# Retention and two FFNs on one core: from the ninth unit on, one attention visit per unit in place of two

## The chip, the cores and the metric

The kernel runs on one core of a Trainium2 chip. The metric is device time of one execution in microseconds (us); before the change it was 1397.0 us, the median of 3 runs (1395.46 to 1397.63).

## What is computed

Everything is fp32. Retention over 8 batches, 8 heads, 576 positions, 64 features a head, then two feed-forward networks over the 4608 tokens of 512 features:

```python
scores = scale * np.matmul(q, k.transpose(0, 1, 3, 2))
gamma = 1.0 - 2.0 ** (-5.0 - np.arange(H))
Dmat = np.where(rel >= 0, gamma[:, None, None] ** rel[None, :, :], 0.0)
x = np.matmul(scores * Dmat, v)          # (B, H, S, D), then tokens x 512
h = x @ w_in                             # 512 -> 2048
x = (h * np.cos(h)) @ w_out              # 2048 -> 512
h = np.maximum(np.maximum(x @ w1, x @ w2), x @ w3)   # 512 -> 768, three times
out = h @ w_out2                         # 768 -> 512
```

## The kernel before

**Tiling.** Tokens are cut into 9 blocks of 512. A *unit* is one block and one pair of heads, so there are 36 units (`NUNIT`), four per block, counted from 0; retention of a unit is worked in chunks of at most 128 positions. The decay factors are taken apart: `v` is scaled by a growing factor beforehand (`att_scale`, GpSimd, for units 3 to 7 ScalarE), the outputs by a falling one afterwards (`att_decay`, VectorE), so that the scores need a 0/1 mask only (`att_mask`, VectorE). What lies before a chunk comes in through a running sum of key-value products: `att_products` (TensorE) makes a unit's products, `att_states` copies them out of PSUM (ScalarE) and adds them to the carried sum (GpSimd). `att_out` makes the outputs: the *inner* part, masked scores times `v` (line 667), and the *outer* part, carried sum times `q` (line 679), both into one PSUM bank `po`. `att_scores` (line 600) makes the scores into two banks `sc`. A unit's data lie in one tile `u`, loaded by `att_load` on SP's queue.

**The FFN beside it.** The FFN products are split in two fp32r halves (`high`, a cast on ScalarE; `low`, the rest, on VectorE, line 399) and use seven products in place of eight (A11, S1, A12, S2, A22, S4, S3). In this phase every FFN product is one *slot* of 12 matmuls of 256 columns (line 422). Each block takes 14 slots; two groups of four weight columns. After a slot its sum is taken by ScalarE (`copy`) or, for S4 and S3, by VectorE (`plus`, line 475). A gate (`gate`: two ScalarE steps, lines 526 and 536, and two VectorE steps, lines 530 and 539) follows each half group. `low` of a block's S2 is issued in the block's slot 1 (slot 14j of block j), two slots before TensorE reads it; those of S4 and S3 two slots later.

**The order** is written out by hand. `at(n, fn, turn)` puts a step on the agenda n slots ahead; `tick()` ends a slot, after its 12 matmuls and its own copy or `plus` have been issued, and then runs what is due: first the steps put down as `AHEAD`, in the order in which they were put down, later the others (`LATER`), in that order too. Each engine's queue is in order. The first 17 slots (`LEAD`) hold the lead-in of weights and units 0 to 7 (`NLEAD` is 8); the slots of the FFN are counted from 0 after them. Unit n from 8 on begins at slot `start_of(n)` = 3 + 11(n-8)//3, so three or four slots apart (3, 6, 10, 14, 17, ...). Units 8 and 9 have loads and scaling of their own.

**The attention steps of a unit n before** (`att_unit`): load at start-4, scaling at start-1, scores at start (`AHEAD`), mask at start+1; at start+5 the visit (`AHEAD`): key-value products of unit n+1 (`att_products(n + 1)`), then inner and outer outputs of unit n (`att_out(n)`), and in the same slot the states of n+1; at start+6 the decay of unit n. So TensorE breaks its FFN matmuls twice per unit: for scores, and one or two slots after the next unit's scores for products and outputs.

After the blocks' first FFN half follow, on the same agenda, the second half of the input weights, the output product, and the second FFN; the change touches none of them. There are 8 PSUM banks: one holds a sum for the whole phase, up to three belong to FFN groups, four to attention (`sc` twice, `kv`, `po`).

Of the kernel before, what the change touches and what calls it, by code (L numbers as in the profile page):

```python
# [39 lines left out]
def chunks_of(j):  # L40

    t0 = j * NB
    cut = (-t0) % S
    segs = [(0, cut), (cut, NB)] if 0 < cut < NB else [(0, NB)]
    out = [(a, min(CH, e - a)) for s, e in segs for a in range(s, e, CH)]
    full = [c for c in out if c[1] == CH]
    short = [c for c in out if c[1] < CH]  # L50
    assert len(short) in (0, 2) and all(n == CH // 2 for _, n in short)
    order = full + short
    col = {a: sum(n for _, n in order[:i]) for i, (a, _) in enumerate(order)}
    return [(a, n, col[a], (t0 + a) % S) for a, n in out]
# [52 lines left out]
def retention_ffn(ctx: ExitStack, tc: tile.TileContext, att, w_in, w_out, w123, w_out2, cst, out):  # L107
# [9 lines left out]
    def w14(name, dt=F32R):  # L117
        shape = [128, 7, 2, HB] if dt == F32R else [128, 7 * NB]
        return wpool.tile(shape, dt, tag="w", name=name)
# [4 lines left out]
    def bank(name):  # L124
        return ps.tile([128, NB], F32, tag="b", name=name)
# [21 lines left out]
    AHEAD, INSIDE, AFTER, LATER = range(4)  # L147

    def at(n, fn, turn=LATER):
        agenda.setdefault(slot[0] + n, [[], [], [], []])[turn].append(fn)  # L150
# [398 lines left out]
    units = {}  # L549
    quarters_of = {}  # L550

    def order_of(n):
        return divmod(n, NPAIR)

    def att_load(n):
        j, hp = order_of(n)
        w = w14(f"u{j}_{hp}", F32)
        units[n] = {
            "qk": w[:, : 2 * NB].rearrange("p (a n) -> p a n", a=2),
            "kv": w[:, 2 * NB : 4 * NB].rearrange("p (a n) -> p a n", a=2),  # L560
            "tv": w[:, 4 * NB : 4 * NB + NTV],
            "ret": w[:, 4 * NB + NTV : 6 * NB + NTV].rearrange("p (a n) -> p a n", a=2),
            "sums": w[:, 6 * NB + NTV : 6 * NB + NTV + 4 * D].rearrange("p (k n) -> p k n", n=D),
            "w": w,
        }
        nc.sync.dma_start(out=w[:, : 4 * NB + NTV], in_=att[j, hp])
# [3 lines left out]
    def att_scale(n):  # L570

        u = units[n]
        v = u["kv"][:, 1].rearrange("p (s d) -> p s d", d=64)
        if n in ON_ACT:
            for s in range(8):
                nc.scalar.mul(v[:, s], v[:, s], u["tv"][:, s : s + 1])
        else:
            nc.gpsimd.tensor_tensor(out=v, in0=v, in1=u["tv"].unsqueeze(2).to_broadcast([128, 8, 64]), op=ALU.mult)
        for _, m, c, pos in chunks_of(order_of(n)[0]):
            if m < CH and pos + m == S:  # L580
                s, p = divmod(c, CH)
                nc.gpsimd.memset(u["kv"][p : p + m, 0, s * CH : (s + 1) * CH], 0.0)

    def att_scores(n):
        u = units[n]
        ch = chunks_of(order_of(n)[0])
        u["sc"] = [bank(f"sc{n}_{e}") for e in range(2)]
        for s in range(NB // CH):
            sl = slice(s * CH, (s + 1) * CH)
            runs = sorted((c, a) for a, _, c, _ in ch if c // CH == s)  # L590
            for e in range(2):
                r = slice(64 * e, 64 * e + 64)

                a = runs[0][1]
                if len(runs) == 1:
                    q = u["w"][r, a : a + CH]
                else:
                    apart = runs[1][1] - a
                    q = u["w"][r, a : a + 2 * apart].rearrange("p (b d) -> p b d", b=2)[:, :, : CH // 2]
                nc.tensor.matmul(u["sc"][e][:, sl], u["qk"][r, 1, sl], q, start=True, stop=True)  # L600
# [20 lines left out]
    def att_products(n):  # L621

        u = units[n]
        ch = chunks_of(order_of(n)[0])
        kn, v = u["kv"][:, 0], u["kv"][:, 1]
        u["kv_sums"] = b = bank(f"kv{n}")
        for k, i in enumerate(grown(n)):
            s = ch[i][2] // CH
            for e in range(2):
                cols = slice(s * CH + 64 * e, s * CH + 64 * e + 64)  # L630
                nc.tensor.matmul(
                    b[64 * e : 64 * e + 64, k * D : (k + 1) * D], kn[:, cols], v[:, cols], start=True, stop=True
                )

    def att_states(n):

        u = units[n]
        j, hp = order_of(n)
        ch = chunks_of(j)
        of = grown(n)  # L640
        su = u["sums"]
        nc.scalar.copy(su[:, : len(of)], u["kv_sums"][:, : len(of) * D].rearrange("p (k n) -> p k n", n=D))
        before = carry[hp][(j + 1) % 2]
        u["state"] = {}
        for i, (_, m, _, pos) in enumerate(ch):
            if pos:
                u["state"][i] = before
            if i not in of:
                continue
            k = of.index(i)  # L650
            dst = carry[hp][j % 2] if i == len(ch) - 1 else su[:, k]
            if pos:
                nc.gpsimd.tensor_tensor(out=dst, in0=before, in1=su[:, k], op=ALU.add)
            elif i == len(ch) - 1:
                nc.gpsimd.tensor_copy(dst, su[:, k])
            before = dst

    def att_out(n):
        u = units[n]
        j, hp = order_of(n)  # L660
        ch = chunks_of(j)
        qT, v = u["qk"][:, 0], u["kv"][:, 1]
        po = u["po"] = bank(f"po{n}")
        for i, (a, m, c, _) in enumerate(ch):
            s = c // CH
            for e in range(2):
                nc.tensor.matmul(
                    po[64 * e : 64 * e + 64, a : a + m],
                    v[:, s * CH + 64 * e : s * CH + 64 * e + 64],
                    u["ret"][:, e, c : c + m],  # L670
                    start=i == 0,
                    stop=False,
                    skip_group_check=True,
                )
        for i, st in u["state"].items():
            a, m, _, _ = ch[i]
            for e in range(2):
                r = slice(64 * e, 64 * e + 64)
                nc.tensor.matmul(
                    po[r, a : a + m], st[r], qT[r, a : a + m], start=False, stop=True, skip_group_check=True  # L680
                )

    def att_decay(n):
        u = units.pop(n)
        j, hp = order_of(n)
        o = quarters_of.setdefault(j, {"name": f"x{j}", "n": NB})
        half = f"k{hp // 2 + 1}"
        if half not in o:
            o[half] = x4(f"{half}_x{j}", [2, NB])
        cuts = sorted({0, HB, NB, (-j * NB) % S} & set(range(NB + 1)))  # L690
        for lo, hi in zip(cuts, cuts[1:]):
            t, cc = divmod(lo, HB)
            g = CGS + hp * 9 + (j * NB + lo) % S // 64
            at_ = (hp % 2) * HB + cc
            nc.vector.scalar_tensor_tensor(
                out=o[half][:, t, at_ : at_ + hi - lo],
                in0=u["po"][:, lo:hi],
                scalar=cs[:, g : g + 1],
                in1=cs[:, CG + hp * HB : CG + hp * HB + hi - lo],
                op0=ALU.mult,  # L700
                op1=ALU.mult,
            )

    def att_visit(n):

        if n + 1 < NUNIT:
            att_products(n + 1)
        att_out(n)

    def att_unit(n, start):  # L710

        if n not in (NLEAD, NLEAD + 1):
            at(max(0, start - 1), lambda: att_scale(n))
        at(start, lambda: att_scores(n), AHEAD)
        at(start + 1, lambda: att_mask(n))
        if not n:
            at(start + 1, lambda: att_products(n), AHEAD)
            at(start + 1, lambda: att_states(n))
        at(start + 5, lambda: att_visit(n), AHEAD)
        if n + 1 < NUNIT:  # L720
            at(start + 5, lambda: att_states(n + 1))
        at(start + 6, lambda: att_decay(n))

    NUNIT = NBLK * NPAIR

# [74 lines left out]
    NLEAD = 8  # L800
# [13 lines left out]
    at(3, claim)  # L814
    at(4, lambda: lead_in(1, 0, nc.vector, nc.vector, SECOND))
    for n in range(NLEAD):
        att_unit(n, 2 * n + 1)
    at(13, lambda: lead_in(2, 0, nc.vector, nc.vector, SPREAD))
    at(16, lambda: lead_in(3, 0, nc.vector, nc.vector, SPREAD))
    build_in(block_of(0), 0, (10, 14, 15, 16), (10, 12, 14, 16, 17, 18, 19), xsd[0], nc.vector)  # L820
# [4 lines left out]
    def start_of(n):  # L825
        return 3 + (11 * (n - NLEAD)) // 3

    for n in range(NLEAD, NUNIT):
        if n > NLEAD + 1:
            at(max(0, start_of(n) - 4), lambda n=n: att_load(n))  # L830
        att_unit(n, start_of(n))
    per = 14
    for j in range(1, NBLK):
        build_in(block_of(j), per * j, (-11, -4, -3, -1), (-10, -8, -3, -1, 1, 1, 4), xsd[j], nc.vector if j == NBLK - 1 else nc.gpsimd)
# [32 lines left out]
    for i in range(4):  # L867
        n = endA + (10, 38, 66, 90)[i]
# [772 lines left out]
```

## Time and profile before

| | us |
|---|---|
| median of 3 runs | 1397.0 (1395.46 to 1397.63) |
| the profiled execution | 1396.5 |
| its span, first to last instruction | 1394.7 |
| TensorE busy in it | 1363.3 |
| VectorE busy | 1129.4 |
| ScalarE busy | 799.0 |
| GpSimd busy | 230.0 |

The retention phase lies in the first 313 us of the span. The profile is of one execution. Engines: PE is TensorE's matmuls, DVE is VectorE, ACT ScalarE, POOL GpSimd, SP the queue that issues loads and stores. A row of the timeline merges neighbouring instructions of a kind: start, length, engine, line, operation, output and inputs by tile name, shapes, count, and in brackets the idle time before it with what ended it. Matmuls are pipelined and the last one's end is modelled, so the time that a group costs TensorE is read from its start to the start of the next row and not from its length.

### The profile page before, as it was taken

How to read it: one execution, taken by the hardware profiler on the slowest of the kernel's cores; microseconds unless marked ns; L12 is line 12 of the kernel's file. 1: busy time of each engine (PE TensorE's matmuls, PEld its weight loads, DVE VectorE, ACT ScalarE, POOL GpSimd, SP SyncE). 2: the span in 40 equal slices, each digit the busy share in tenths (PEclk: the TensorE clock that was granted, in tenths of full speed). 3: DMA queues.
4: the chain of work that ended last, by engine and by line, in shares of the span. 5: the costliest groups of instructions: out<-in, count | busy, mean ns of one | idle time of the engine just before them, and what ended most of it. 6: DMA issues, size and time to landing. Idle time of an engine off the chain costs nothing.

```text
span 1394.7 us, 22899 instructions
## 1 busy us (share of the span) xinstructions
PE 1363.3 (98%) x8794; PEld 1175.4 (84%) x8794; DVE 1129.4 (81%) x1471; ACT 799.0 (57%) x1238; POOL 230.0 (16%) x259
## 2 busy tenths in 40 slices
PE   7899999999999999999999999999999999999998
PEld 5799999998888887888988888889878888888887
DVE  8988878989687789989879989577777567868884
ACT  6565565568677876666456556444544434444553
POOL 4455555730110000000011110100100000000000
PEclk9999999999999999999999999999999999999999
DMA  9679899988999975664577997343434476255633
GB/s 387 249 286 333 332 343 311 340 314 318 357 349 339 358 286 211 242 226 173 178 258 207 309 255 209 100 154 114 174 134 159 166 273 252 88 180 155 224 106 121
DMA packets 113085, 333.67 MB, mean 239 GB/s; under 512 B 9936, under 2 KB 18256, under 8 KB 107344
## 3 DMA queue, kind: packets, MB, share of 16 engines
q1 hardware_dynamic: 110096, 322.77, 63.9%
q0 software_dynamic: 2880, 9.44, 3.7%
q8 instruction: 69, 1.13, 0.3%
q14 instruction: 40, 0.33, 0.1%
HBM read 194.28 MB, written 137.89 MB: 238 GB/s over the span
## 4 chain that ended last, share of the span: by engine, by line
PE 55%; DMA 5%; DVE 3%; ACT 1%; issue 1%; SPq 0%; ACTq 0%; DVEq 0%
PE d_e L444 12%; PE d_g L976 11%; PE b_g L976 6%; PE b_e L444 6%; PE d_u L1506 5%; PE a_g L976 3%; PE a_e L444 3%; PE b_u L1506 2%; PE d_b L422 2%; PE a_u L1506 1%; DMA mqp<-ext 1%; PE b_b L422 1%; PE d_gs L976 1%; DMA gqp<-s_a 1%; DMA ar_b<-w 1%
## 5 line engine op out<-in xcount | busy, mean ns | idle before, releaser
L976 PE MATMUL d_g<-h_g,w_wo 128*128 128x512 f32 x512 | 157.9, 390 | 0.5 <-ACT o_g L999 0.5
L444 PE MATMUL in<-y,w_wi 128*128 128x512 f32 x672 | 153.0, 389 | 0.0
L444 PEld LDWEIGHTS in<-y,w_wi 128*128 128x128 f32 x672 | 125.9, 188 | 26.5 <-ACT s_a L1112 0.4
L943 DVE TENSOR_TENSOR l_g<-q_g,h_g 128x1024 fp32r<-128x1024 f32 x96 | 116.7, 1229 | 13.9 <-ACT h_g L936 9.5
L469 ACT ACTIVATE ext<-d_e 128x512 f32<-128x512 f32 x72 | 43.1, 599 | 143.1 <-PE d_e L444 143.1
L422 PE MATMUL d_a<-x_x,w_wi 128*128 128x256 f32 x864 | 117.3, 288 | 7.1 <-DVE w_wi L236 4.8
L936 ACT CAST h_g<-q_g 128x1024 fp32r<-128x1024 f32 x96 | 99.0, 1052 | 35.3 <-DVE q_g L927 22.9
L422 PEld LDWEIGHTS d_a<-x_x,w_wi 128*128 128x128 f32 x864 | 107.7, 192 | 12.3 <-DVE w_wi L236 5.0
L976 PEld LDWEIGHTS d_g<-h_g,w_wo 128*128 128x128 f32 x512 | 95.9, 188 | 20.6 <-ACT o_g L999 0.9
L539 DVE SCALAR_TENSOR_TENSOR s_a<-t_a,s_a 128x1024 f32<-128x1024 f32 x68 | 94.1, 1385 | 12.0 <-ACT t_a L536 12.0
L976 PE MATMUL d_g<-l_g,w_wo 128*128 128x512 f32 x256 | 99.8, 390 | 0.2 <-DVE l_g L943 0.2
L530 DVE SCALAR_TENSOR_TENSOR t_a<-s_a,t_a 128x1024 f32<-128x1024 f32 x68 | 88.5, 1303 | 14.2 <-ACT t_a L526 14.2
L526 ACT ACTIVATE t_a<-s_a 128x1024 int32<-128x1024 f32 x68 | 71.9, 1058 | 21.5 <-DVE s_a L1115 15.3
L536 ACT ACTIVATE t_a<-t_a 128x1024 f32<-128x1024 f32 x68 | 72.0, 1059 | 20.5 <-DVE t_a L530 20.2
L444 PE MATMUL d_e<-h_e,w_b 128*128 128x512 f32 x304 | 81.4, 390 | 0.8 <-DVE ext L473 0.8
L976 PE MATMUL b_g<-h_g,w_wo 128*128 128x512 f32 x256 | 79.2, 390 | 1.5 <-ACT h_g L936 1.5
L473 DVE TENSOR_TENSOR ext<-ext,b_e 128x512 f32<-128x512 f32 x36 | 24.7, 686 | 59.4 <-PE b_e L444 51.7
L444 PEld LDWEIGHTS d_e<-h_e,w_b 128*128 128x128 f32 x304 | 56.9, 188 | 12.9 <-DVE ext L473 1.2
L422 PE MATMUL b_a<-x_x,w_wi 128*128 128x256 f32 x432 | 60.6, 290 | 0.9 <-DVE x_x L399 0.9
L976 PEld LDWEIGHTS b_g<-h_g,w_wo 128*128 128x128 f32 x256 | 47.8, 188 | 12.1 <-ACT h_g L936 2.4
L422 PEld LDWEIGHTS b_a<-x_x,w_wi 128*128 128x128 f32 x432 | 55.3, 195 | 3.2 <-DVE x_x L399 1.1
L976 PEld LDWEIGHTS d_g<-l_g,w_wo 128*128 128x128 f32 x256 | 48.1, 188 | 11.0 <-DVE l_g L943 1.0
(371 smaller groups left out, 3322.4 us busy)
## 6 DMA issues: line engine op xcount, KB each, us to landing
u<-att SPq DMA_DIRECT2D x36, 1028.0 KB, 8.3
gqp<-s_a SPq DMA_DIRECT2D x64, 512.0 KB, 6.8
q_g<-gqp SPq DMA_DIRECT2D x64, 512.0 KB, 7.0
xsp<-x_x SPq DMA_DIRECT2D x56, 512.0 KB, 7.5
y<-xsp SPq DMA_DIRECT2D x56, 512.0 KB, 8.8
mqp<-ext SPq DMA_DIRECT2D x24, 512.0 KB, 4.1
st_b<-p_b SPq DMA_DIRECT2D x21, 512.0 KB, 6.4
w_b<-st_b SPq DMA_DIRECT2D x5, 1792.0 KB, 12.8
```

The lines of the kernel that those rows point to most:

```text
L422: nc.tensor.matmul(h[:, p * HB : (p + 1) * HB], a, b, start=first and p == 0 and i == 0, stop=i == len(terms) - 1, skip_group_check=True,)
L444: nc.tensor.matmul(dst, a, b, start=first and i == 0, stop=i == len(terms) - 1, skip_group_check=True)
L469: nc.scalar.activation(dst, b[:, :n], AF.Copy, scale=scale)
L473: nc.vector.tensor_tensor(out=dst, in0=dst, in1=b[:, :n], op=ALU.add)
L526: nc.scalar.activation(st["t"], s, AF.Copy, bias=0.25)
L530: nc.vector.scalar_tensor_tensor(out=r, in0=s, scalar=MOST_TURNS, in1=st["t"], op0=ALU.min, op1=ALU.subtract)
L536: nc.scalar.activation(r, r, AF.Sin, scale=TURN, bias=HALF_PI)
L539: nc.vector.scalar_tensor_tensor(out=s, in0=f32(st["t"]), scalar=-1.0, in1=s, op0=ALU.max, op1=ALU.mult)
L936: nc.scalar.copy(h, ts[i][q])
L943: nc.vector.tensor_tensor(out=lo, in0=t, in1=f32(h), op=ALU.subtract)
L976: nc.tensor.matmul(to, a, v[:, p].rearrange("p (b n) -> p b n", b=2) if half and n == 2 else v[:, :, r], start=first and k == 0 and p == 0 ...
L1506: nc.tensor.matmul(dst, a, v, start=first and p == 0 and i == 0 and (wide or mt == 0), stop=p == 2 and i == 2, skip_group_check=True,)
```

## The change

`att_out` is cut in two, `att_inner` and `att_outer`. A visit at slot `start` of unit n now holds, in this order, scores of n (from unit 8 on), inner outputs of n-1, key-value products of n, outer outputs of n-1. Units 0 to 7 keep their scores in a slot of their own and their visit in the slot in which it was (2n + 4, for unit 0 slot 2), with inner outputs now ahead of products. From unit 8 on decay of n-1, mask of n and states of n are put down for start+1, in this order in each engine's queue; before, decay stood at the unit's own start+6, which is one or two slots later than now, products and states at the unit before's start+5, which is one or two slots (products) or none or one slot (states) later. Scaling goes from start-1 to start-2, the load from start-4 to start-5. Outputs of the last unit get a visit of their own, at the slot where a unit 36 would begin.

```diff
-    def att_out(n):
+    def att_inner(n):
         u = units[n]
-        j, hp = order_of(n)
-        ch = chunks_of(j)
-        qT, v = u["qk"][:, 0], u["kv"][:, 1]
+        ch = chunks_of(order_of(n)[0])
+        v = u["kv"][:, 1]
         po = u["po"] = bank(f"po{n}")
         for i, (a, m, c, _) in enumerate(ch):
...
+
+    def att_outer(n):
+        u = units[n]
+        ch = chunks_of(order_of(n)[0])
+        qT, po = u["qk"][:, 0], u["po"]
         for i, st in u["state"].items():
...
     def att_visit(n):
 
-        if n + 1 < NUNIT:
-            att_products(n + 1)
-        att_out(n)
-
-    def att_unit(n, start):
+        if n >= NLEAD:
+            att_scores(n)
+        if n:
+            att_inner(n - 1)
+        att_products(n)
+        if n:
+            att_outer(n - 1)
+
+    def att_unit(n, start, visit):
 
         if n not in (NLEAD, NLEAD + 1):
-            at(max(0, start - 1), lambda: att_scale(n))
-        at(start, lambda: att_scores(n), AHEAD)
+            at(max(0, start - (1 if n < NLEAD else 2)), lambda: att_scale(n))
+        if n < NLEAD:
+            at(start, lambda: att_scores(n), AHEAD)
+        at(visit, lambda: att_visit(n), AHEAD)
+        if n:
+            at(visit + 1, lambda: att_decay(n - 1))
         at(start + 1, lambda: att_mask(n))
-        if not n:
-            at(start + 1, lambda: att_products(n), AHEAD)
-            at(start + 1, lambda: att_states(n))
-        at(start + 5, lambda: att_visit(n), AHEAD)
-        if n + 1 < NUNIT:
-            at(start + 5, lambda: att_states(n + 1))
-        at(start + 6, lambda: att_decay(n))
+        at(visit if n < NLEAD else visit + 1, lambda: att_states(n))
...
     for n in range(NLEAD):
-        att_unit(n, 2 * n + 1)
+        att_unit(n, 2 * n + 1, 2 * n + 4 if n else 2)
...
     for n in range(NLEAD, NUNIT):
         if n > NLEAD + 1:
-            at(max(0, start_of(n) - 4), lambda n=n: att_load(n))
-        att_unit(n, start_of(n))
+            at(max(0, start_of(n) - 5), lambda n=n: att_load(n))
+        att_unit(n, start_of(n), start_of(n))
+    at(start_of(NUNIT), lambda: (att_inner(NUNIT - 1), att_outer(NUNIT - 1)), AHEAD)
+    at(start_of(NUNIT) + 1, lambda: att_decay(NUNIT - 1))
```

## Rows read from the trace of the kernel before

**Rows 1.** The page, part 1: busy us (share of the span) and instructions of an engine.
```profile
PE 1363.3 (98%) x8794; PEld 1175.4 (84%) x8794; DVE 1129.4 (81%) x1471; ACT 799.0 (57%) x1238; POOL 230.0 (16%) x259
```

**Rows 2.** Waits of PE over the span: line, waited for, us, times, longest.
```profile
PE sc L600 <- DMA u<-att: 9.5, 2, 8.2
PE d_a L422 <- DVE w_wi L236: 4.8, 1, 4.8
PE d_a L422 <- DVE x_x L399: 2.2, 2, 1.8
...
PE b_a L422 <- DVE x_x L399: 0.9, 1, 0.9
```

**Rows 3.** Timeline of PE, 241 to 262 us: units 28 to 30, block 6.
```profile
244.49 1.16 PE L600 MATMUL sc<-u 64*128 64x128 f32 x16
245.58 1.70 PE L422 MATMUL b_a<-x_x,w_wi 128*128 128x256 f32 x12
247.21 0.69 PE L631 MATMUL kv<-u 128*64 128x64 f32 x16
...
249.63 3.13 PE L422 MATMUL d_a<-x_x,w_wi 128*128 128x256 f32 x24
252.69 1.16 PE L600 MATMUL sc<-u 64*128 64x128 f32 x16
...
259.27 2.89 PE L422 MATMUL d_a<-x_x,w_wi 128*128 128x256 f32 x22
```

**Rows 4.** Timeline of PE, 44 to 51 us: the second visit of unit 7, unit 8's scores.
```profile
45.68 0.57 PE L631 MATMUL kv<-u 128*64 128x64 f32 x12
...
47.88 1.16 PE L600 MATMUL sc<-u 64*128 64x128 f32 x16
48.97 1.69 PE L422 MATMUL b_a<-x_x,w_wi 128*128 128x256 f32 x12
```

**Rows 5.** Timeline of PE, 199 to 206 us: a second visit of the same size.
```profile
202.66 0.57 PE L631 MATMUL kv<-u 128*64 128x64 f32 x12
...
204.87 1.70 PE L422 MATMUL sums<-x_x,w_wi 128*128 128x256 f32 x12
```

**Rows 6.** Timeline of DVE, 56 to 60.5 us: decay of unit 7, sums, weight split.
```profile
56.69 0.99 DVE L695 SCALAR_TENSOR_TENSOR k_x<-po,cs 128x64 f32<-128x64 f32 x3
57.60 0.41 DVE L210 TENSOR_TENSOR s_wi<-fa_wi 128x256 f32<-128x256 f32 x1
...
59.06 0.68 DVE L236 TENSOR_TENSOR w_wi<-fa_wi,w_wi 128x512 fp32r<-128x512 f32 x1
```

**Rows 7.** Stretches, PE: stretch, us, busy us (matmuls), granted clock, DMA share, GB/s.
```profile
60.00:65.00 5.00, 5.00 (x29) 0.50 0.27 107
```

**Rows 8.** Timeline of DVE, 246.5 to 262 us: slots 81 to 86.
```profile
247.32 0.69 DVE L475 SCALAR_TENSOR_TENSOR s_a<-b_a,s_a 128x512 f32<-128x512 f32 x1 [1.35 <-PE b_a L422]
...
254.18 2.06 DVE L539 SCALAR_TENSOR_TENSOR s_a<-t_a,s_a 128x1024 f32<-128x1024 f32 x1
...
257.49 1.44 DVE L399 TENSOR_TENSOR x_x<-tb_x,x_x 128x512 fp32r<-128x512 f32 x1
...
260.11 0.99 DVE L695 SCALAR_TENSOR_TENSOR k_x<-po,cs 128x256 f32<-128x256 f32 x3
```

**Rows 9.** Timeline of DVE, 75 to 92 us: slots 11 to 17.
```profile
75.64 0.69 DVE L475 SCALAR_TENSOR_TENSOR s_a<-b_a,s_a 128x512 f32<-128x512 f32 x1
...
85.54 0.68 DVE L399 TENSOR_TENSOR x_x<-tb_x,x_x 128x512 fp32r<-128x512 f32 x1
...
91.11 1.22 DVE L539 SCALAR_TENSOR_TENSOR s_a<-t_a,s_a 128x1024 f32<-128x1024 f32 x1
```

**Rows 10.** Timeline of DVE, 311 to 314 us: the last unit's decay.
```profile
312.51 0.88 DVE L695 SCALAR_TENSOR_TENSOR k_x<-po,cs 128x256 f32<-128x256 f32 x2 [1.43 <-PE po L679]
```

**Rows 11.** Timeline of POOL, 284 to 292 us: scaling of unit 34.
```profile
289.20 2.02 POOL L578 TENSOR_TENSOR u<-u 128x512 f32<-128x512 f32 x1
```

**Rows 12.** Timeline of PE, 288 to 294 us: products of unit 34.
```profile
292.39 0.57 PE L631 MATMUL kv<-u 128*64 128x64 f32 x12
```

## The prediction

> **What bounds the kernel now.** I read the page first: TensorE is busy for 98% of the span and VectorE for 81% [rows 1], so time is gained where TensorE's own stream gets shorter, and lost again where VectorE makes it wait. Then the waits of TensorE: in all of the retention phase it waits 4.8 us once for split weights, 2.2 and 0.9 us for low halves of operands, and for a unit's load only in the lead, before the ninth unit [rows 2]. So behind the lead this phase is one unbroken row of matmuls, and its length is what they cost from start to start. That is read from TensorE's timeline of one unit of the middle [rows 3]: the reader is to see 12 or 24 FFN matmuls (one or two slots), then a scores visit, a slot, the second visit, two slots, and so on. Last I followed VectorE through the same stretch [rows 8], since its queue is strictly in order and the change puts its work for a unit together. The phase lies before everything else, and TensorE is the bound behind it too, so what is won at its end I carry to the end of the kernel in full.
>
> **The change, part by part.** Slots are counted from 0 at the first FFN slot of block 0; "unit 8" is the ninth.
>
> *Fewer breaks in the FFN stream.* One slot between two visits takes 1.63 us (245.58 to 247.21), two slots between two visits 3.06 us (249.63 to 252.69) [rows 3]. An undisturbed slot is thus 1.43 us, and going into one visit and coming out of another costs 0.20 us together. Before, the stream is broken for the scores of units 8 to 35 and for the second visits of 7 to 35; unit 8's scores already stand behind unit 7's second visit, so there are 56 breaks. After, there are 28 joint visits, and the outputs of unit 35 alone: 29. So 27 breaks fewer, 27 x 0.20 = 5.4 us. All matmuls stay. Inside the visit, the step from scores to inner outputs is not in the trace. The nearest row is the one joint visit that there is: 45.68 to 48.97, 3.29 us [rows 4], against 1.09 us for scores (244.49 to 245.58) [rows 3] and 2.21 us for the same second visit standing alone (202.66 to 204.87) [rows 5], 3.30 us together. So I take the inside at no change. Bounds: products to inner outputs need no change of array shape, so the new step may cost less than the one in that row, or more; with three quarters of a break (0.15 us) a unit either way the term is 1.3 to 9.5 us.
>
> The Trainium skill (TensorEngine Tiling (Array Packing), Key Properties) says that a change of tiling mode drains the array. The joint visit has four such changes (full array, 64 rows by 128 columns, 128 by 64, 64 by 64, full) where the two have five, so by that rule too one goes per unit. Counting the drain as the way in alone (an estimate, half of the 0.20), the sum of this term would be 2.7 us; the rows have the way out in them as well, and I go by the rows.
>
> *Start of the phase.* VectorE is behind here: TensorE waits 4.8 us [rows 2] for the weight split that starts at 59.06. Ahead of it in VectorE's queue stands the decay of unit 7, 56.69 to 57.60, 0.91 us [rows 6]. After, this decay is put on the agenda by unit 8, so in its slot it comes behind the sums and the split. The wait ends 0.9 us earlier: 0.9 us gained. What TensorE does next needs the mask of unit 8, which keeps its place, and the second visit of unit 8 moves into time in which the rest of the split was waited for, so I don't see it given back. After that idle time the granted clock stood at 0.50 from 60 to 65 [rows 7], the lower level of 1.2 GHz. If the shorter idle time lets it stand at 2.4 GHz, up to 2 us more goes (5 us at half clock hold 2.5 us of work, less what waits on VectorE anyway); I don't count on it.
>
> *Bunched work on VectorE.* Decay of the last unit and mask of this one now stand one behind the other, one slot after the visit, where they lay one or two slots apart. In front of both stands that slot's own sum, if it is a slot in which VectorE adds a product (the S4 and S3 slots); it needs that slot's matmuls, and these now come behind a visit of 3.3 to 3.5 us. Behind the two stand the low halves of the next block, of which S2's is issued two slots before TensorE reads it. So I followed each block from the last sum for which VectorE waits to the low half of S2. The hardest is block 6 (units 29 and 30). Before: VectorE starts at 247.32 and ends that low half at 257.49 + 1.44 = 258.93, 11.6 us [rows 8]; TensorE comes to its slot at 259.27 [rows 3] and needs it four matmuls (0.48 us) later: 0.8 us to spare. After: the slot in front of the sum comes behind the joint visit, so from the end of it TensorE has slots of 1.43 and 1.53, a visit of 1.09 + 2.42 (247.21 to 249.63), slots of 1.53 and 1.43 and 0.48 us: 9.9 us. VectorE needs 0.1 + 11.6 + 0.9 us, since the decay that stood at 260.11 [rows 8] now comes before. TensorE waits 2.7 us. Two rows in the stretch are long: the gate's product took 2.06 us, against 1.22 us for the same at 91.11 [rows 9], and the low half 1.44 against 0.68 us (85.54) [rows 9]. At the short lengths, with smaller excesses in the rows between, VectorE is about 2.1 us quicker and 0.6 us of waiting is left. I take 2.0 us, nearer to the measured rows.
>
> The Trainium skill (SBUF — State Buffer, Who interferes with whom) says that a VectorE instruction with two SBUF inputs and a GpSimd instruction that reads SBUF shut each other out for a whole instruction, whichever starts first. The long rows fit it, and by it their lengths in the new order aren't those of the old: by the rule this term can be anything from 0.6 to 2.7 us.
>
> Block 1 (unit 10) in the same way: from 75.64 to 85.54 + 0.68 is 10.6 us [rows 9], from the end of the slot TensorE has 1.43 + 1.43 + 1.53 + 3.3 + 1.53 + 0.48 = 9.7 us: 1.0 us of waiting with these rows, none at short lengths; I take 0.7 us. In blocks 2 to 5 my sums come out within some tenths on either side: 0.3 us in all. At the end of the phase VectorE idled 1.43 us for the last decay (312.51) [rows 10], with TensorE then waiting for its low halves [rows 2]; this decay comes two slots earlier, so 0.5 us of that comes back. Sum 2.5 us lost, 0 to 6 as bounds.
>
> *Loads, scaling, states, banks.* The load of a unit is issued a slot earlier, and the tile that it reuses is set free one or two slots earlier, so SP's queue is held no longer behind it. Scaling moves one slot forward, products one or two: on GpSimd the closest case ended at 289.20 + 2.02 = 291.22 before products at 292.39 [rows 11, 12], 1.2 us. After, the states' copy on ScalarE stands one slot behind the products, GpSimd's additions wait for it, and the next scaling is behind them; but from products to products lie three or four full slots and a whole visit, 7.8 us or more (3.3 + 3 x 1.43 + 0.2), and copy, additions and scaling end in time by my sum. Cost 0; if the cover is gone, some tenths in each of the eight units with three slots, up to 3 us. The mask is read one or two slots sooner; by the walk of block 6 it is done about 1 us before. The visit takes four PSUM banks at once; those of the unit before were given back two slots earlier: 0.
>
> **Sum**, against the profiled execution's 1396.5 us (span 1394.7; the median shown is 1397.0): 1396.5 - 5.4 - 0.9 + 2.5 = 1392.7 us.
>
> **Rivals.** *VectorE keeps pace*: the long rows fall away in the new order and the waits with them; for it speaks that these lengths depend on what GpSimd does at the time, against it that GpSimd's work is as much as before. 1396.5 - 6.3 = 1390, and 1388 if the clock stays up at the start. *Even*: blocks 1 and 6 wait by the long rows and GpSimd's chain adds a microsecond: 1396.5 - 6.3 + 5.5 = 1396. *VectorE decides* (slower): where the sum of a slot stands behind the visit, VectorE idles through 5 us and then has a sum, a decay, a mask and a gate step before the low halves, so that every block loses what block 6 loses. It decides from 6.3 / 8 = 0.8 us a block; at the long-row bound of block 6 in half of the blocks and 0.7 us in the rest, 4 x 2.7 + 4 x 0.7 = 13.6 us, it gives 1396.5 - 6.3 + 13.6 = 1404; at 1.2 us a block 1400. Against it: in blocks 2 to 5 and 7 the sums show slack.
>
> **How the numbers follow.** Forecast (1390.5 to 1395.5) 0.55; VectorE keeps pace 0.17; even 0.15; VectorE decides 0.13. The time is the forecast's, 1392.7. The range takes in the second and third case and the beginning of the fourth: 1388.5 to 1399.5. A measurement tells 0.2%, 2.8 us, from no change, so faster is below 1394.2: 0.38 of the forecast's 0.55 and all of the second, 0.55; slower, above 1399.8, 0.13; the rest 0.32.
>
> **What would show it.** In the timeline: 28 joint visits of about 3.3 to 3.5 us, undisturbed slots between them, and 0.20 us less per unit. The wait for split weights near 59 us shorter by 0.9 us. In the waits of TensorE low halves (x_x) as new entries, one of 1 to 3 us in block 6 and up to one near 87 us in block 1; none for GpSimd's scaling. In VectorE's timeline the decay right ahead of the mask. I am wrong if the visits get longer inside by more than 0.1 us, if products wait for scaling, or if low halves are waited for in most blocks.

## The result and the profile after

The changed kernel takes **1405.85 us** (median of 5 runs, 1402.36 to 1409.43) against 1397.63 us before (5 runs): ratio 1.0060, interval 1.0037 to 1.0083. It is slower by 8.2 us. The forecast was 1392.7 us and the range ended at 1399.5; the time is that of the rival with a chance of 0.13, "VectorE decides". The profiled execution of after took 1402.36 us, its span is 1400.6 us. It is the fastest of the five, so some 2.4 us of the 8.2 lie outside what the two profiles show. Behind line 655 the line numbers of after differ: inner outputs are line 666, outer ones 683, the decay 699, later lines up to 8 higher.

The page of after, part 1. TensorE, ScalarE and GpSimd are busy as long as in [rows 1], within 3 us; VectorE is busy 8.9 us longer with the same 1471 instructions.

```profile
PE 1362.7 (97%) x8794; PEld 1179.6 (84%) x8794; DVE 1138.3 (81%) x1471; ACT 796.4 (57%) x1238; POOL 231.7 (17%) x259
```

The difference shows when the span is cut at the same FFN work: the first matmul of slot 9 (behind the lead) and the first of slot 113 (the end of the retention phase). Stretches of PE, first before, then after; columns: stretch, its length, busy us (instructions) of PE, PEld, DVE, ACT and POOL, granted TensorE clock, DMA share, GB/s.

```profile
69.75:319.69 249.94, 249.89 (x2894) 232.57 (x2893) 217.78 (x330) 152.15 (x242) 133.45 (x154) 1.00 0.87 316
```

```profile
69.45:327.46 258.01, 248.24 (x2895) 234.36 (x2894) 225.14 (x327) 150.75 (x244) 137.60 (x156) 0.99 0.87 307
```

The phase, as these stretches are called from here on, is 8.1 us longer. TensorE's idle time in it (length less busy) went from 0.05 to 9.77 us, while its busy time fell by 1.65 us. The change does what it says, and something else takes back more. The waits of TensorE over the span (us, times, longest), against [rows 2]:

```profile
...
PE d_a L422 <- DVE x_x L399: 9.4, 5, 2.7
PE d_a L422 <- DVE w_wi L236: 3.0, 1, 3.0
PE b_a L422 <- DVE x_x L399: 2.3, 3, 1.2
...
PE sums L422 <- DVE x_x L399: 1.7, 2, 0.9
```

Waits for low halves (x_x) were 3.1 us and are 13.4 us: 10.3 us more, and 9.4 of the 13.4 lie in the phase. The largest are one per block, in blocks 4, 5 and 6; they end at 191.10 (shown below) and here:

```profile
229.79 1.21 PE L422 MATMUL d_a<-x_x,w_wi 128*128 128x256 f32 x8 [2.70 <-DVE x_x L399]
```

```profile
266.70 1.57 PE L422 MATMUL d_a<-x_x,w_wi 128*128 128x256 f32 x11 [1.96 <-DVE x_x L399]
```

In the kernel before, the profile lists no wait of TensorE for a low half between 66 and 320 us.

Block 4 shows how one arises. VectorE's timeline of after (start, us, instruction; in brackets idle time before it):

```profile
178.96 0.69 DVE L475 SCALAR_TENSOR_TENSOR s_a<-b_a,s_a 128x512 f32<-128x512 f32 x1
...
180.46 1.59 DVE L197 SCALAR_TENSOR_TENSOR ar_wi<-ar_wi 128x512 uint32<-128x512 uint32 x1
181.97 2.29 DVE L530 SCALAR_TENSOR_TENSOR t_a<-s_a,t_a 128x1024 f32<-128x1024 f32 x1
...
185.63 0.99 DVE L699 SCALAR_TENSOR_TENSOR k_x<-po,cs 128x256 f32<-128x256 f32 x3
186.54 1.40 DVE L609 TENSOR_TENSOR u<-sc,cs 128x384 f32<-128x384 f32 x4
187.87 1.73 DVE L539 SCALAR_TENSOR_TENSOR s_a<-t_a,s_a 128x1024 f32<-128x1024 f32 x1
189.52 1.52 DVE L399 TENSOR_TENSOR x_x<-tb_x,x_x 128x512 fp32r<-128x512 f32 x1
```

TensorE's timeline of the same time:

```profile
187.99 0.64 PE L422 MATMUL d_a<-x_x,w_wi 128*128 128x256 f32 x4
191.10 1.88 PE L422 MATMUL d_a<-x_x,w_wi 128*128 128x256 f32 x8 [2.47 <-DVE x_x L399]
192.91 2.03 PE L600 MATMUL sc<-u 64*128 64x128 f32 x16
```

From 179.87 on VectorE runs without a gap (0.23 us of idle time lie ahead of that); the low half ends at 191.04 and the matmul starts at once. The decay (185.63) stands right ahead of the mask (186.54), as forecast. But four rows in the stretch are long: 1.59 us (line 197), 2.29 (530), 1.73 (539) and 1.52 (399). In block 4 of the kernel before, line 197 took 0.69 us (181.62) and the other three these times:

```profile
182.23 1.22 DVE L530 SCALAR_TENSOR_TENSOR t_a<-s_a,t_a 128x1024 f32<-128x1024 f32 x1
...
186.15 1.34 DVE L539 SCALAR_TENSOR_TENSOR s_a<-t_a,s_a 128x1024 f32<-128x1024 f32 x1
...
188.32 0.88 DVE L399 TENSOR_TENSOR x_x<-tb_x,x_x 128x512 fp32r<-128x512 f32 x1
```

So the four rows grew by 0.9 + 1.1 + 0.4 + 0.6 = 3.0 us, more than the wait of 2.5 us. GpSimd in the same stretch of after:

```profile
177.87 2.08 POOL L578 TENSOR_TENSOR u<-u 128x512 f32<-128x512 f32 x1
...
180.05 1.45 POOL L391 TENSOR_TENSOR tb_x<-k_x,ta_x 128x512 f32<-128x512 f32 x1
181.46 1.72 POOL L391 TENSOR_TENSOR ta_x<-k_x,k_x 128x512 f32<-128x512 f32 x1
183.14 2.02 POOL L203 TENSOR_TENSOR ar_wi<-ar_wi 128x512 uint32<-128x512 uint32 x1
```

Its subtractions (line 391) run while VectorE runs lines 197 and 530; a third one (187.21 to 188.51) and a scaling (line 578, 188.47 to 190.50) lie beside the two later long rows. In the kernel before, VectorE idled for the same sum, and the first subtraction and half of the scaling (line 578) fell into that idle time; VectorE first, then GpSimd, both of before:

```profile
179.33 0.69 DVE L475 SCALAR_TENSOR_TENSOR s_a<-b_a,s_a 128x512 f32<-128x512 f32 x1 [2.58 <-PE b_a L422]
```

```profile
177.56 1.29 POOL L391 TENSOR_TENSOR tb_x<-k_x,ta_x 128x512 f32<-128x512 f32 x1
178.84 1.05 POOL L578 TENSOR_TENSOR u<-u 128x512 f32<-128x512 f32 x1
```

Line 197, which has two inputs in SBUF, shows the same from 66 to 320 us; instructions, then shortest/median/longest ns. First before, then after:

```profile
L197 DVE SCALAR_TENSOR_TENSOR ar_wi<-ar_wi x7: 692/693/694, 78.0 to 181.6; 128x512 uint32<-128x512 uint32 x7
L197 DVE SCALAR_TENSOR_TENSOR ar_wo<-ar_wo x6: 692/693/694, 202.1 to 285.2; 128x512 uint32<-128x512 uint32 x6
```

```profile
L197 DVE SCALAR_TENSOR_TENSOR ar_wi<-ar_wi x7: 692/694/1591, 80.6 to 180.5; 128x512 uint32<-128x512 uint32 x7
L197 DVE SCALAR_TENSOR_TENSOR ar_wo<-ar_wo x6: 692/695/1805, 206.3 to 294.9; 128x512 uint32<-128x512 uint32 x6
```

Right behind the wait of 2.5 us the clock fell to its lower level, 1.2 GHz, for 3.4 us, 1.7 us of time; the scores at 192.91 took 2.03 us in place of 1.16. The stretch of after:

```profile
191.35:194.77 3.42, 3.42 (x24) 3.12 (x23) 2.04 (x3) 1.54 (x2) 0.00 (x0) 0.50 0.28 105
```

The account of the profiled phase: +9.7 us idle, +1.7 us clock, and what remains of +8.1 us is -3.4 us for the breaks. Outside the phase after is 0.3 us quicker at the start and 1.9 us behind slot 113. There the two kernels do the same work, and in the first FFN's output product TensorE waited 5.3 us for halves of its operands before (lines 936 and 943) and 2.5 us after; over the kernels profiled here, with the same code in that part, these waits are 2.5 to 5.3 us, so it is not shown to be an effect of the change.

### The profile page after: what moved, and what is told of

The parts are those of the page before. It is cut to its first block, busy times and chain, and to the rows that moved or that the text cites. A ratio compares the mean times of both kernels' runs of the same rounds, so it can differ in the third digit from the quotient of the medians.

```text
span 1400.6 us, 22834 instructions
## 1 busy us (share of the span) xinstructions
PE 1362.7 (97%) x8794; PEld 1179.6 (84%) x8794; DVE 1138.3 (81%) x1471; ACT 796.4 (57%) x1238; POOL 231.7 (17%) x259
## 4 chain that ended last, share of the span: by engine, by line
PE 66%; DVE 5%; DMA 4%; ACT 2%; issue 1%; SPq 0%; POOL 0%; DVEq 0%; ACTq 0%
PE d_e L444 13%; PE d_g L984 11%; PE in L444 9%; PE b_e L444 6%; PE b_g L984 6%; PE d_u L1514 5%; PE a_e L444 3%; PE a_g L984 3%; PE b_u L1514 2%; PE d_b L422 2%; PE a_u L1514 1%; PE b_b L422 1%; DMA gqp<-s_a 1%; PE d_a L422 1%; PE d_gs L984 1%
## 5 line engine op out<-in xcount | busy, mean ns | idle before, releaser
L984 PEld LDWEIGHTS b_g<-h_g,w_wo 128*128 128x128 f32 x256 | 47.9, 188 | 10.3 <-ACT h_g L944 0.6
```

Source lines behind the costliest of these rows:

```text
L984: nc.tensor.matmul(to, a, v[:, p].rearrange("p (b n) -> p b n", b=2) if half and n == 2 else v[:, :, r], start=first and k == 0 and p == 0 ...
```

## The experiments

Theories of the loss: **A**, the merged visit puts decay and mask together and the low halves behind them come late by VectorE's own queue; **B**, GpSimd's work now runs beside VectorE's tight stretch and holds it off; a third, that the earlier scaling and loads do it. In the expectations the letters are given anew for each run. All medians are of 10 runs unless said, each beside runs of the kernel before (medians 1396.9 to 1397.7); ratios are against these. After itself has five runs, so a difference from it is known to some 3 us either way. Only the edit is shown.

**The decay back at its old slot** (on after).

```
-            at(visit + 1, lambda: att_decay(n - 1))
+            at(visit + 1 if n <= NLEAD else start_of(n - 1) + 6, lambda: att_decay(n - 1))
-    at(start_of(NUNIT) + 1, lambda: att_decay(NUNIT - 1))
+    at(start_of(NUNIT - 1) + 6, lambda: att_decay(NUNIT - 1))
```

> The changed kernel, with one step moved back: from unit 9 on the decay of a unit is put down for the slot in which it stood before the change (its own start+6, one or two slots behind the joint visit's own slot + 1). Theory A (bunching: decay and mask in front of the low halves make TensorE wait): in blocks 4, 5 and 6 the stretch from the S4 sum to the low half of S2 loses 0.9 us of VectorE work, so the waits for low halves in blocks 3 to 7, 9.2 us together in the changed kernel, fall to 5 or 6 us, and the time to about 1400 us. Theory B (GpSimd's work falls into VectorE's tight stretch and lengthens its instructions): waits stay at 8 to 10 us, time 1403 to 1408 us.

1401.7 us, ratio 1.0024 (1.0007 to 1.0040). The waits of TensorE from 66 to 320 us:

```profile
PE d_a L422 <- DVE x_x L399: 4.1, 3, 2.0
PE kv L631 <- DVE k_x L699: 1.7, 2, 1.1
```

Waits for low halves fall from 9.4 us (of after in the same stretch) to 4.1, those of blocks 3 and 7 go and little is left of block 6's; in blocks 4 and 5 two of about 2 us stay. By the medians the place of the decay in VectorE's queue is half of the loss (4.1 of 8.2 us; by the spread of the runs 1.8 to 7.3), not all of it.

**Scaling and loads one slot earlier, alone** (on before).

```
-            at(max(0, start - 1), lambda: att_scale(n))
+            at(max(0, start - (1 if n < NLEAD else 2)), lambda: att_scale(n))
-            at(max(0, start_of(n) - 4), lambda n=n: att_load(n))
+            at(max(0, start_of(n) - 5), lambda n=n: att_load(n))
```

> The kernel before, with only the load and the scaling of units 10 to 35 one slot earlier, as the change has them; two visits per unit stay. Theory B (order and time of GpSimd's work): long instructions on VectorE in front of the low halves of blocks 4 and 5 and new waits of TensorE of 1 to 3 us each, time 1399 to 1403 us. Theory A: no new waits over 0.5 us, time as before, 1396 to 1398 us.

1398.4 us, ratio 1.0013 (1.0001 to 1.0026), waits for low halves 0.8 us in the phase. By itself this part of the change costs 0.6 us by the medians and 1.8 by the ratio, 3.6 at the end of its interval: not the loss, though perhaps a part.

**GpSimd's subtractions taken out**, on after and, as control, on before (writes of zeros in their place, so that this part of the computation is left out; there are four per block, not six as one expectation says).

```
+        if eng is nc.gpsimd:
+            eng.memset(d, 0.0)
+        else:
+            eng.tensor_tensor(out=d, in0=a, in1=b, op=ALU.subtract)
```

> The changed kernel without the differences that GpSimd takes of the retention outputs of blocks 1 to 7: in their place GpSimd writes zeros, which reads nothing, so this part of the computation is left out. Theory B: without GpSimd's longest instructions the VectorE rows in front of the low halves go back to their short lengths (gate steps 1.2 us, low half 0.7 us), waits for low halves in blocks 3 to 7 fall from 9.2 us to under 2 us, time 1391 to 1395 us. Theory A: the rows that stand in front stay, waits of 1 us or more remain in blocks 4 to 6, 4 to 6 us together, time 1399 to 1402 us.

> The kernel before, with GpSimd's six subtractions per block of the low operands (blocks 1 to 7) replaced by writes of zeros: that part of the computation is left out, as in no_minus. Control for no_minus, which gave 1394.6 (3.1 us under the kernel before, 11.2 under the changed kernel). Theory A: GpSimd's work costs time only where the merged visit puts it beside VectorE's steps that bound the low halves; the kernel before waits 0.2 us in all for low halves between 66 and 320 us, so it gains nothing: 1395.5 to 1399. Theory B: less work on GpSimd is worth 3 us or more in any kernel: 1391 to 1395, and no_minus then says little of the merge.

On after 1394.6 us, 0.9969 (0.9954 to 0.9983): 11.2 us less. On before 1395.3 us, 0.9989 (0.9976 to 1.0001): 1.5 us less by the ratio, between 3.4 us less and none. In the phase the low halves of the former are waited for 2.3 us:

```profile
PE d_a L425 <- DVE x_x L402: 1.5, 3, 0.8
PE sums L425 <- DVE x_x L402: 0.8, 1, 0.8
```

So without these four instructions per block the merged schedule keeps pace with its control, and the interplay of the two is the loss: theory B, on top of A. The pages of the four kernels say what the interplay is. With the same 1471 instructions VectorE is busy 1129.4 us before and 1116.3 without the subtractions, 1138.3 after and 1121.8 without them. So with them it is busy 13.1 us longer in the kernel before too, and 16.5 after; most of the long rows are not new, but in the new order they stand where a low half is due. (The zeros also change what TensorE multiplies; the next run keeps the values.)

**The subtractions on VectorE** (on after). This tells A from B, since VectorE gets more to do.

```
-..., xsd[j], nc.vector if j == NBLK - 1 else nc.gpsimd)
+..., xsd[j], nc.vector)
```

> The changed kernel with the four subtractions per block of blocks 1 to 7 done by VectorE in place of GpSimd, at the same slots; nothing else. VectorE gets 4 x some 0.7 us a block, 20 us in all, more to do; GpSimd loses about 45 us. Theory A (VectorE's own work, bunched by the merged visit, is what makes the low operands late): the waits for low halves, 10 us between 66 and 320 us, grow by 1 to 3 us a block: 1408 to 1425. Theory B (GpSimd's subtractions hold VectorE's operations with two inputs off for as long as they run, 1.2 to 1.8 us each, more than VectorE would need for the same work): the rows of the 128x1024 VectorE products fall from 2.1-2.3 to about 1.2 us, the waits shrink to 2 to 6 us: 1395 to 1402.

1400.0 us, 1.0024 (1.0011 to 1.0037), 5.8 us less than after (2.8 to 8.3 by the spread of the runs), though VectorE has more work. The gate's product (line 539) in the phase, after and then this kernel (busy us, mean ns, idle before it):

```profile
L539 DVE SCALAR_TENSOR_TENSOR s_a<-t_a,s_a 128x1024 f32<-128x1024 f32 x28 | 42.2, 1507 | 6.6 <-ACT t_a L536 6.5
```

```profile
L539 DVE SCALAR_TENSOR_TENSOR s_a<-t_a,s_a 128x1024 f32<-128x1024 f32 x29 | 38.2, 1318 | 3.0 <-ACT t_a L536 3.0
```

The waits for low halves halve, to 4.7 us:

```profile
PE d_a L422 <- DVE x_x L399: 4.2, 3, 2.0
PE kv L631 <- POOL u L578: 1.4, 1, 1.4
PE b_a L422 <- DVE x_x L399: 0.5, 1, 0.5
```

A alone is refuted: more work on VectorE made it faster. Block by block the profiled executions of the two edits part the theories. The wait of block 6 is 1.96 us in after, 0.17 with the decay back and again 1.96 with the subtractions on VectorE: there the queue's order decides, as the prediction had it. Those of blocks 4 and 5 are 2.47 and 2.70 in after, 1.92 and 1.99 with the decay back, 0.73 and 1.51 with the subtractions moved: there GpSimd has the larger part. How much of what stays is owed to GpSimd's other work, scaling above all, no run tells.

**Low operands one slot earlier** (with their casts and three of the four subtractions), on after, and as control on before (there in blocks 1 to 7 only, on after in block 8 too).

```
-        build_in(..., (-11, -4, -3, -1), (-10, -8, -3, -1, 1, 1, 4), ...
+        build_in(..., (-11, -5, -4, -2), (-10, -8, -4, -2, 0, 0, 3), ...
```

> The changed kernel with the operands of blocks 1 to 8 made one slot earlier from the second difference on (casts and low halves of A12, S2, S4, S3 and A22, and the differences they need). Theories A and B both say that a burst of VectorE work is in front of a deadline: with one slot (1.43 us) more the waits for low halves in blocks 3 to 7 fall from 9.2 us to under 2 us and the time to 1391 to 1396 us, under the kernel before. Theory C (VectorE lacks time over the whole phase, not in bursts): the waits move along and stay at 7 us or more, time over 1402 us.

> The kernel before with the low operands of blocks 1 to 7 made one slot earlier, by the same new offsets as low_early. Theory A: the earlier operands only take away waits that the merged visit brought (9 to 10 us in the changed kernel, 0.2 us in the kernel before), so here they bring nothing: 1395.5 to 1400, with new waits of up to 2 us where the earlier operands meet the decay of the block's last unit. Theory B: the earlier operands are a gain of their own, 3 to 4 us as in low_early: 1393 to 1395, and the merge then gains nothing by itself.

On after 1394.0 us, 0.9981 (0.9968 to 0.9994): 11.9 us less. On before 1395.3 us, 0.9983 (0.9971 to 0.9995): 2.4 us less by the ratio, between the two theories of its expectation. No low half is waited for in the merged kernel's phase any more; 3 us of small waits (a sum's copy, scaling, masks) are left. The largest of them, 1.2 us at 189.04, is for a sum's copy on ScalarE; one expectation below takes it for a low half's. That stretch also holds the plainest pair of rows. VectorE at 183.20, and GpSimd beside it:

```profile
183.20 3.08 DVE L197 SCALAR_TENSOR_TENSOR ar_wi<-ar_wi 128x512 uint32<-128x512 uint32 x1
```

```profile
183.22 1.27 POOL L391 TENSOR_TENSOR ta_x<-k_x,k_x 128x512 f32<-128x512 f32 x1
184.45 1.27 POOL L391 TENSOR_TENSOR tb_x<-tb_x,k_x 128x512 f32<-128x512 f32 x1
```

0.69 us of work took 3.08 us: the excess, 2.39 us, is about GpSimd's two instructions, 2.5 us from 183.22 to 185.72. Here the low half had lead enough, and TensorE did not wait for it.

**Both: earlier operands (blocks 1 to 7) and the decay back**, on after.

> The changed kernel with both edits: low operands of blocks 1 to 7 one slot earlier, and the decay products at the slot where the kernel before had them. Alone they gave 1394.0 and 1401.7 against 1405.9. Theory A (both take load off the same stretch of VectorE, the earlier operands being the larger part): the last wait of low_early, 1.3 us at 189.0 in block 4, goes, no other comes: 1391 to 1394.5. Theory B: with the operands one slot earlier, the decay put back stands ahead of the first group's low operands again, as in the kernel before, and delays them: two or more waits of over 1 us, 1395 to 1399.

1396.8 us, 0.9998 (0.9985 to 1.0011), 2.8 us more than the earlier operands alone. The two remedies don't add. The time is in the range of the expectation's second theory, but not by its mechanism. The new waits are, by the releaser that the profile names, for the decay itself, behind which the bank of the outputs is free again; for a low half there is none from 66 to 320 us:

```profile
PE kv L631 <- DVE k_x L699: 2.8, 4, 1.0
PE b_a L422 <- DVE k_x L699: 1.8, 1, 1.8
```

**The price of a break** (on low_early): the scores get a visit of their own again, one slot ahead.

```
     def att_visit(n):
-        if n >= NLEAD:
-            att_scores(n)
...
-        if n < NLEAD:
-            at(start, lambda: att_scores(n), AHEAD)
+        at(start - (n >= NLEAD), lambda: att_scores(n), AHEAD)
```

> low_early with the scores of each unit from the ninth on in a visit of their own, one slot ahead of the rest: the second visit per unit is back, all else of the change stays. It gives the price of a break of the FFN stream alone. Theory A (a break costs 0.19 to 0.20 us, as the starts of the matmuls around a visit read): 27 breaks more, 5.1 to 5.4 us, 1398 to 1400.5. [...] Theory C (a break costs nothing, the gain of low_early over the kernel before is in its operands): 1393 to 1395.

1399.5 us, 1.0013 (0.9998 to 1.0028): 5.5 us more than low_early, as its theory A says. The phase (slot 9 to slot 113) of low_early, then of this kernel:

```profile
71.94:321.49 249.55, 246.57 (x2894) 233.29 (x2893) 227.28 (x328) 150.42 (x245) 138.31 (x156) 1.00 0.89 319
```

```profile
68.37:323.32 254.95, 251.43 (x2894) 234.75 (x2893) 224.89 (x328) 150.74 (x245) 139.22 (x156) 1.00 0.88 313
```

5.4 us longer, 4.9 of them busy time with the same matmuls: 0.19 us for each of the 26 breaks in this stretch. The two profiled executions took the same time, 1396.8 us, since that of low_early came 3.6 us later to slot 9; over the kernels here slot 9 begins anywhere from 67 to 72 us, so single spans don't tell the price, the stretch and the medians do.

**Scaling yet one slot earlier** (on low_early; scaling at `start - 3`, loads at `start_of(n) - 6`).

> low_early with the scaling of a unit's values three slots ahead of its visit in place of two, and its load six slots ahead in place of five. Theory A: key-value products that wait for the scaling (0.4 at 202.5, 0.5 at 238.7 in low_early) no longer do; 1 us less, 1392 to 1394. Theory B: the scaling moves into the stretch in which the subtractions stand, and another low operand comes late: 1394.5 to 1398.

1394.5 us, 0.9974 (0.9964 to 0.9984), against 1394.0: no difference.

**Both remedies that held, and their control.** Earlier operands and subtractions on VectorE, on after (measured twice, 4 and 10 runs) and on before (12 runs; blocks 1 to 7).

> low_early (1394.0; waits of 4.7 us left in the phase against a merged phase without waits) with the four subtractions per block on VectorE. Theory A (VectorE's own load): waits grow by 5 us or more, 1399 to 1412. Theory B (GpSimd holds VectorE off): of the 4.7 us left, those for low operands (1.3 at 189) and for scaling on GpSimd (0.4 to 0.8 each at 202.5 and 238.7) go: 1389.5 to 1393.5.

> low_early_all_vector once more beside its control, for the ratio. Theory A: 1390 to 1392, 4 to 6 us under the control. Theory B: within 1.5 us of the control.

> The kernel before with both edits of low_early_all_vector: low operands of blocks 1 to 7 one slot earlier, their subtractions on VectorE; two visits per unit as before. Control for low_early_all_vector (1391.0). Theory A (the merged visit is worth its 26 breaks of 0.19 us and the earlier start once its waits are covered; the edits by themselves bring the 0 to 2 us that before_low_early and before_no_minus showed): 1394.5 to 1398. Theory B (the edits are the gain, the merge brings nothing even where it is covered): 1390 to 1392.5.

The merged one: 1391.0 us, 0.9951 (0.9936 to 0.9967), and 1391.9 us, 0.9958 (0.9942 to 0.9973). It beats both kernels, by 5 to 6 us and by some 14. The control: 1393.9 us, 0.9976 (0.9963 to 0.9988). So 3.0 us come from the edits without the merge, and 2.0 us from the merge (with the earlier operands of block 8, which the control lacks); the intervals of the two overlap, so that the latter could be anywhere from nothing to 4 us. Neither theory of the control hit it, and of the repeated run the first had the time right but not the 4 to 6 us of difference. In the three pairs with equal edits the merged kernel is 0.6 us (without subtractions), 1.3 (earlier operands) and 2.0 us quicker than its control: the saved breaks show in the phases, but no pair gives more than a part of the 5.4 us. The phase of the control and of the merged one:

```profile
68.79:318.23 249.44, 249.44 (x2895) 232.47 (x2893) 222.15 (x357) 150.54 (x242) 92.45 (x127) 1.00 0.90 317
```

```profile
67.05:315.02 247.97, 245.62 (x2894) 232.72 (x2893) 225.22 (x357) 150.62 (x245) 98.82 (x128) 1.00 0.91 321
```

3.8 us less busy time, 0.15 us for each of the 26 breaks, and 2.35 us of new idle time, of which 2.0 us is for scaling on GpSimd:

```profile
PE kv L631 <- POOL u L578: 2.0, 3, 0.9
```

## Why the prediction was wrong, step by step

- **Fewer breaks, -5.4 us: right in kind, somewhat large.** Three pairs of phases, with 26 of the 27 breaks in them, give 3.4, 3.8 and 4.9 us of busy time; the whole difference of medians with the break put back is 5.5 us. The joint visit takes 3.3 us as forecast (81.63 to 84.90). The sum by the drain alone, worked out from the Trainium skill (TensorEngine Tiling (Array Packing), Key Properties), was 2.7 us; every pair lies above it.
- **Start of the phase, -0.9 us: the mechanism came, the gain at slot 9 is not settled.** From the matmuls ahead of the wait to those behind it passed 6.72 us before and 5.83 after, 0.89 us less. Before, then after:

```profile
53.08 1.93 PE L422 MATMUL d_a<-x_x,w_wi 128*128 128x256 f32 x14 [1.77 <-DVE x_x L399]
59.80 1.65 PE L422 MATMUL d_a<-x_x,w_wi 128*128 128x256 f32 x6 [4.79 <-DVE w_wi L236]
```

```profile
54.22 2.87 PE L422 MATMUL d_a<-x_x,w_wi 128*128 128x256 f32 x14 [1.77 <-DVE x_x L399]
60.05 1.65 PE L422 MATMUL d_a<-x_x,w_wi 128*128 128x256 f32 x6 [2.96 <-DVE w_wi L236]
```

The pair with both remedies gives 6.24 and 5.33. But this execution came to the first of the two rows 1.14 us later, so the wait ended 0.25 us later than before, and the split itself began at 59.30 against 59.06 [rows 6]. That the wait shrank by 1.8 us says little: TensorE came to it 2.1 us later. The hoped-for clock gain did not come; in the profiled execution of after the clock stood at its lower level from 54.8 to 65, longer than before.
- **Bunched work on VectorE, +2.5 us: the step that failed.** The mechanism was named; its size was 10.3 us of waits and 1.7 us of clock behind one of them, outside the bound of 6 as well. The sign set for it, low halves waited for in most blocks, came: in blocks 3 to 7. Block 6 was forecast at 2.0 us and waits 1.96 us. Block 1 was forecast at 0.7 us and waits for nothing. What failed is the sentence that blocks 2 to 5 come out "within some tenths on either side": TensorE's waits there are 0.9 us in block 3, 2.5 in block 4 and 2.7 in block 5, and block 7, given slack, waits 1.2 us. I walked those blocks with the row lengths of the kernel before. In block 4 VectorE took 9.9 us from the sum to the low half of S2 (179.33 to 189.20), with two decays in it; with one, as in after, that is 9.0 us, and TensorE allowed it 9.7 (178.96 to 188.63). It took 12.1 us (178.96 to 191.04): in the new order GpSimd's operations lie beside other VectorE rows, which grow by 0.4 to 1.1 us each. The Trainium skill's page SBUF — State Buffer, Who interferes with whom, was cited for this in block 6 and priced there at 0.6 to 2.7 us; it should have been applied to every block, as a bound of each one. By the 2.7 us in blocks 3 to 6 and 0.7 in the others the walk would have ended at about 1404, which is the rival's sum. That this lies near the measured time is partly luck: it stands on 13.6 us of waits, and 10.3 were measured.
- **End of the phase, -0.5 us: wrong by about a microsecond.** The four slots from slot 113 on take 8.75 us in after (327.46 to 336.21) and 8.05 before (319.69 to 327.74), 0.7 us more in place of 0.5 less. The last decay was put down two slots earlier, but VectorE came to it only at 320.13, 7.3 us ahead of slot 113, as before (312.51, 7.2 us).
- **Loads, scaling, states and banks, 0: nearly right in after** (0.6 us of waiting for scaling in all), but the version with both remedies loses 2.0 us to scaling, within the 3 us set as the bound.
- **The chances.** "VectorE decides" got 0.13 on the ground that the sums of most blocks showed slack. That slack was a few tenths, against rows known to vary by 0.8 us. Its text counts the steps in VectorE's queue, which block 6 bears out; the rows that grew in blocks 4 and 5 it does not name.

What stays open: why both edits together make even the two-visit kernel 3 us faster. Its profiled span is 4.2 us shorter: 1.0 us ahead of slot 9, 0.5 in the phase and 2.7 behind slot 113, where the code is the same and the waits in the output product, 5.3 and 3.3 us, differ from kernel to kernel anyway. Open too are the 2.4 us by which the medians differ more than the profiled executions.

## What to carry to other kernels

When steps of an in-order engine are put closer together, walk every stretch with the longest length that each row has anywhere in the trace, not with the length it has at its present place: the neighbour that stretches it moves too. Before merging visits to save breaks, look at what the second engine has to spare per block; here a slot more of lead for its results and four instructions moved off GpSimd took the waits away, and of the breaks' saving 2 us were left, with nothing to 4 us as bounds. An instruction moved from a slower engine onto a fuller one can make the fuller one quicker, if the two shut each other out.

## What the runs showed of the hardware

- A VectorE instruction beside GpSimd's subtractions took 3.08 us in place of 0.69, the excess being the length of the two GpSimd instructions. The Trainium skill (SBUF — State Buffer, Who interferes with whom) says that such instructions shut each other out for a whole instruction; these rows agree in the length. Which of the two began first they can't tell: their starts are 0.02 us apart, VectorE's ahead.
- The clock fell to 1.2 GHz for 3.4 us right behind a wait of TensorE of 2.5 us (after, 191.10 and 191.35), and 1 to 2 us behind two waits of about 2 us (decay_back). The wait of 2.7 us in block 5 of after was followed by no fall. The median over the runs of the mean granted clock was 0.993 for after and 0.993 to 0.994 for decay_back and all_vector, the kernels with several such waits, against 0.996 for the kernel before and 0.995 for low_early and no_minus. At 1.4 us per thousandth (an estimate from 1400 us) at most some 4 of the 8.2 us are clock: at most, since a low clock costs nothing while TensorE waits. That is a reading of these means, not an experiment.

The stretches of decay_back behind its two waits:

```profile
191.80:195.20 3.40, 3.40 (x42) 3.18 (x41) 3.40 (x8) 1.36 (x2) 0.00 (x0) 0.50 0.40 60
229.30:232.70 3.40, 3.40 (x29) 2.94 (x29) 3.24 (x5) 1.65 (x2) 0.00 (x0) 0.50 0.86 309
```
